# Other durations, latencies and keys for the planner of a fused attention and mixture-of-experts kernel, and one conversion step on another engine

## The chip, the cores and the metric

The kernel runs on one core of one Trainium2 chip. The metric is the time of one execution on the device, in microseconds: the median of 3 runs before the change is 2100.59 us (2096.8 to 2104.3).

The core has a matrix engine (TensorE, PE in the profile), which writes to PSUM only, a vector engine (VectorE, DVE), a scalar engine (ScalarE, ACT), GpSimd (POOL), and SyncE (SP), whose queue issues all DMAs here. Each engine takes its instructions strictly in the order in which the program lists them, and waits on semaphores for the others.

## The reference

Three layers follow one another, all in float32:

```
scores = scale * q k^T;  bias = -(cum[:, None] - cum[None, :]), cum = cumsum(max(s, 0))
attn   = softmax(causal(scores + min(bias, 0)));   x = attn v         # 4 x 8 heads, 576 x 64
P      = exp(x w_gate - max);  8 times: rows, then columns normalised # 2304 tokens, 8 experts
out    = sum over e of P[:, e] * (max(x w1[e], 0) w2[e])              # 512 -> 1024 -> 512
y      = leaky(out w_in) w_out,  leaky(h) = max(0.01 h, h)            # 512 -> 2048 -> 512
```

`w_in` and `w_out` come as float64 and are turned into float32 on the chip.

## The kernel before

**Exact products.** A float32 operand is split into a high part, rounded to the matrix engine's own format by a copy on ScalarE, and a low part, the difference, which VectorE or GpSimd subtracts. Each product then takes three matmuls: high by high, high by low, low by high (lines 294 to 296 for the first layer of an expert, 1054 to 1056 and 1269 to 1271 for the second).

**Seven products for eight.** The first layer of a block (a quarter of an expert's hidden width, 256 columns, on 2 x 384 tokens) is a 2 x 2 block product in the form with seven multiplications P1 to P7. Sums of blocks of the weights and of the inputs go in; additions on VectorE between PSUM banks (line 976, tiles `Uu`, `sc`, `FB`) combine the products afterwards. TensorE starts on a PSUM bank's next product only when these additions have been done.

**Stages.** Attention comes first. Then tokens are taken in three passes (j = 0, 1, 2). A pass runs through 32 units, a unit being a quarter of one of 8 experts. After the three passes, three FF passes of 8 units each compute the last layer. Units are numbered through: 0 to 31 for the first pass, 32 to 63 and 64 to 95 for the second and third, 96 to 119 for the FF passes.

- In the first pass each unit's weights are loaded and split (`weights1`, `weights2`, lines 225 to 277), used, and also stored to DRAM: the seven first-layer operands to `w1c`, the split second-layer blocks to `w2d`, and the unsplit sums of second-layer blocks (`sums`, line 272) to `w2s`. Gating (lines 864 to 935) runs beside units 0 to 3: TensorE computes logits, ScalarE copies them (line 913), TensorE transposes them (line 868), and VectorE normalises.
- From unit 32 on the second layer uses seven products as well. Its operands come from DRAM: `fetch1` (line 1206) brings first-layer operands, `fetch2` (lines 1248 and 1250) second-layer ones. The four that are sums arrive unsplit and `round2` splits them: a cast on ScalarE (line 1255), a subtraction on VectorE (line 1256). There are five buffers, so a fetch waits for the use of the buffer five places earlier. `comb` (line 1230) combines the results of the first layer and `split` (1235 and 1236) splits them, the low parts on GpSimd. `tile2` multiplies and adds to accumulators in `X` (line 1277); `merge` (line 1285) joins these at the end of a pass.
- `conversion` (lines 949 to 956) turns one 128 x 512 piece of `w_in` or `w_out` from float64 bits into float32 by eight VectorE operations. 32 pieces are spread over units: 19 over the first pass from unit 4 on, 13 over the second pass.
- `prepare(u)`, eight times during the third pass, loads a block of the converted `w_in`, forms and splits the first-layer operands, stores them to `w1c`, then does the same with `w_out` for `w2d` and `w2s`. Its VectorE operations stand at line 1355 (a helper) and 272, its casts at 1363, 1367, 1368 and 1378.

**The order of the work.** All that follows attention goes through one planner, `Flow`. `do(engine, key, dur, emit, reads, writes, lat)` adds a task; a task depends on the last writers of what it reads, and on readers and writers of what it writes, by names such as `("w1c", n)`. These names serve the planner; the program's semaphores come from the memory that is touched. `order()` simulates the engines: whenever an engine is free, it takes the ready task with the smallest key. A task is ready when its dependencies have ended and their latency has passed (a table by pair of engines, or `lat` in ns). `dur` is an estimate in ns; `pd`, `pq`, `pa`, `pgg` and `kb` give it from the number of elements (VectorE on SBUF, VectorE reading PSUM, ScalarE, GpSimd, DMA in KB). TensorE's durations are doubled while the plan's clock is under `KEYS["cold"]` = 28 us. A key is in units of the numbering above: 34.5 is the middle of unit 34. The list that results is the order of each engine's queue.

```
now, eng = best
k = min((j for j, (a, _) in enumerate(ready[eng]) if a <= now), key=lambda j: ready[eng][j][1][1])
...
pd = lambda n: 103.0 + n * 1.042
pq = lambda n: 130.0 + n * 1.12
pa = lambda n: 160.0 + n / 1.2
pgg = lambda n: 92.0 + n * 2.3
```

Of the kernel before, what the change touches and what calls it, by code (L numbers as in the profile page):

```python
# [8 lines left out]
F32 = mybir.dt.float32  # L9
# [14 lines left out]
class Plan:  # L24
# [7 lines left out]
    def __init__(self, free=()):  # L32
        self.tasks, self.free = [], dict(free)
# [80 lines left out]
def fused_kernel(ctx: ExitStack, tc: tile.TileContext, q, k, v, s, w_gate, w1, w2, w_in, w_out, out):  # L114
    nc = tc.nc
# [132 lines left out]
    def weights2(n, key):  # L248
# [657 lines left out]
    def gating():  # L906
# [32 lines left out]
    def convert(bits):  # L939
# [9 lines left out]
            lambda: v_.tensor_scalar(out=cva, in0=hi, scalar1=0x7FFFFFFF, scalar2=None, op0=AND),  # L949
# [9 lines left out]
    def conversion(n, key, unit):  # L959
# [6 lines left out]
        for k, f in enumerate(convert(bits)):  # L966
            do("dve", key + 0.11 * k, (370, 370, 370, 370, 640, 370, 640, 640)[k] + 500, f, [br, ("begun", unit)], ["cv"] if k < 7 else ["cv", br])
# [19 lines left out]
    def first(n):  # L987
# [11 lines left out]
        def out(block, bank, key):  # L999
# [37 lines left out]
    def second(n):  # L1037
# [4 lines left out]
        for ch in range(6):  # L1042
# [22 lines left out]
            elif e == 0:  # L1065
                do("dve", k2, pd(512), lambda a=a, y=y: nc.vector.tensor_tensor(out=a, in0=y, in1=a, op=ALU.add), [yr], [ar])
            else:
# [3 lines left out]
                do("dve", k2, pd(512), lambda a=a, y=y, p=p: nc.vector.scalar_tensor_tensor(out=a, in0=y, scalar=p, in1=a, op0=ALU.mult, op1=ALU.add),  # L1071
# [20 lines left out]
    CONVS = {4 + n: 1 for n in range(25) if n % 4 != 3}  # L1092
# [109 lines left out]
    def fetch1(n, o, t):  # L1202
# [3 lines left out]
        do("sp", t, kb(820 if o < NG else 256), lambda: nc.sync.dma_start(out=to.bitcast(F32), in_=src), [("w1c", ci)], [name], 2000)  # L1206
# [36 lines left out]
    def fetch2(q, n, name, t):  # L1243
# [5 lines left out]
        else:  # L1249
            do("sp", t, kb(512), lambda: nc.sync.dma_start(out=to, in_=w2d[ci // 2][:, part - 4]), [("w2d", ci), ("w2d", ci + 1)], names, 2000)  # L1250
# [96 lines left out]
    def prepare(u, t):  # L1347
# [11 lines left out]
        wr = [("w1c", NU1 + u)]  # L1359
        do("sp", t - 0.5, kb(512), lambda: nc.sync.dma_start(out=rawc, in_=win32[:, 256 * u:256 * u + 256].rearrange("(c p) f -> p c f", p=128)), [("in", 4 * c + u // 2) for c in range(4)], [R], 2000)  # L1360
# [4 lines left out]
        do("sp", t + 0.5, kb(512), lambda: nc.sync.dma_start(out=dst[:, 1:5, 0], in_=hf.rearrange("p o k f -> p o (k f)")), [H], wr, 2000)  # L1365
        do("sp", t + 0.5, kb(512), lambda: nc.sync.dma_start(out=dst[:, 1:5, 1], in_=sw.rearrange("p (o f) -> p o f", o=4)), [S_], wr, 2000)
# [4 lines left out]
        do("sp", t + 0.9, kb(256), lambda: nc.sync.dma_start(out=dst[:, 0:6:5, 0], in_=hf[:, 0:2].rearrange("p o k f -> p o (k f)")), [H], wr, 2000)  # L1371
        do("sp", t + 0.9, kb(128), lambda: nc.sync.dma_start(out=dst[:, 6, 0], in_=hf[:, 2].rearrange("p k f -> p (k f)")), [H], wr, 2000)
        for o, src in ((0, A(0, 0)), (5, A(0, 1)), (6, A(1, 1))):
            do("sp", t + 0.9, kb(128), lambda o=o, src=src: nc.sync.dma_start(out=dst[:, o, 1].rearrange("p (k f) -> p k f", k=2), in_=src), [R], wr, 2000)
        raw2 = raw.rearrange("p (c f) -> p c f", c=2)
        do("sp", t + 1.2, kb(512), lambda: nc.sync.dma_start(out=raw2, in_=wout32[256 * u:256 * u + 256, :].rearrange("(c p) f -> p c f", p=128)), [("out", 2 * u + x) for x in range(2)], [R], 2000)
# [9 lines left out]
    for n in range(N0, N1):  # L1386
# [102 lines left out]
```

## Time and profile before

| | before |
|---|---|
| median of 3 runs | 2100.59 us (2096.8 to 2104.3) |
| the profiled execution | 2099.05 us, span 2097.3 us |
| TensorE busy | 2020.6 us, 96% |
| VectorE busy | 1706.9 us, 81% |
| GpSimd busy | 1689.2 us, 81% |
| ScalarE busy | 906.4 us, 43% |
| mean granted TensorE clock | 0.990 |

The span runs from the first to the last instruction of one profiled execution; the execution's own time is a little longer. Busy time of TensorE counts overlapping matmuls once, and a matmul that waits in the pipe counts as busy. How fast TensorE really goes is therefore read from the number of matmuls that pass in a stretch. The granted clock is a share of 2.4 GHz; 0.5 is 1.2 GHz. In the rows, "DVE X L1 <- ACT Y L2" means that VectorE's instruction of line 1, which writes X, waited for ScalarE's of line 2.

### The profile page before, as it was taken

How to read it: one execution, taken by the hardware profiler on the slowest of the kernel's cores; microseconds unless marked ns; L12 is line 12 of the kernel's file. 1: busy time of each engine (PE TensorE's matmuls, PEld its weight loads, DVE VectorE, ACT ScalarE, POOL GpSimd, SP SyncE). 2: the span in 40 equal slices, each digit the busy share in tenths (PEclk: the TensorE clock that was granted, in tenths of full speed). 3: DMA queues.
4: the chain of work that ended last, by engine and by line, in shares of the span. 5: the costliest groups of instructions: out<-in, count | busy, mean ns of one | idle time of the engine just before them, and what ended most of it. 6: DMA issues, size and time to landing. Idle time of an engine off the chain costs nothing. (4 is left out here: it accounts for less than half of the span.)

```text
span 2097.3 us, 34707 instructions
## 1 busy us (share of the span) xinstructions
PE 2020.6 (96%) x11473; PEld 1904.9 (91%) x11473; DVE 1706.9 (81%) x2987; ACT 906.4 (43%) x1896; POOL 1689.2 (81%) x1607
## 2 busy tenths in 40 slices
PE   7999899999999999999999999999999999999998
PEld 5776688888888899999999989989999999999997
DVE  5877489899888879989998988888888885857746
ACT  5888333333332343333333444333333345555553
POOL 7789877888888668888888978777778797978874
PEclk9999999999999999999999999999999999999999
DMA  6664878888889677778776778888888877776663
GB/s 149 139 143 103 307 251 286 290 318 291 298 293 321 231 254 247 250 245 268 247 249 225 245 268 288 285 281 263 294 280 293 277 242 237 234 241 210 221 213 106
DMA packets 303424, 518.17 MB, mean 247 GB/s; under 512 B 81868, under 2 KB 189550, under 8 KB 287886
## 3 DMA queue, kind: packets, MB, share of 16 engines
q1 hardware_dynamic: 303246, 515.96, 74.7%
q8 instruction: 92, 1.51, 0.3%
q14 instruction: 86, 0.70, 0.1%
HBM read 362.11 MB, written 144.05 MB: 241 GB/s over the span
## 5 line engine op out<-in xcount | busy, mean ns | idle before, releaser
L294 PE MATMUL sc<-XO,WQ 128*128 128x384 f32 x960 | 328.3, 342 | 29.7 <-DVE Uu L976 21.6
L295 PE MATMUL sc<-XO,WQ 128*128 128x384 f32 x960 | 323.8, 337 | 0.0
L296 PE MATMUL sc<-XO,WQ 128*128 128x384 f32 x960 | 323.0, 337 | 0.0
L1256 DVE TENSOR_TENSOR WQ<-WQ 128x512 fp32r<-128x512 f32 x176 | 190.7, 1083 | 71.5 <-ACT WQ L1255 71.1
L294 PEld LDWEIGHTS sc<-XO,WQ 128*128 128x128 f32 x960 | 181.6, 189 | 46.7 <-DVE Uu L976 27.6
L295 PEld LDWEIGHTS sc<-XO,WQ 128*128 128x128 f32 x960 | 182.0, 190 | 4.6
L296 PEld LDWEIGHTS sc<-XO,WQ 128*128 128x128 f32 x960 | 182.0, 190 | 0.0
L1255 ACT CAST WQ<-WQ 128x512 fp32r<-128x512 f32 x176 | 109.2, 621 | 162.4 <-DMA WQ<-w2s 143.2
L1277 DVE TENSOR_TENSOR X<-tr,X 128x384 f32<-128x384 f32 x275 | 149.6, 547 | 33.4 <-PE tr L1271 33.1
L294 PE MATMUL FA<-XO,WQ 128*128 128x384 f32 x480 | 161.7, 337 | 0.5 <-DVE GG L1221 0.5
L296 PE MATMUL FA<-XO,WQ 128*128 128x384 f32 x480 | 160.9, 335 | 0.7 <-POOL WQ L225 0.7
L295 PE MATMUL FA<-XO,WQ 128*128 128x384 f32 x480 | 161.1, 336 | 0.0
L976 DVE TENSOR_TENSOR sc<-sc,Uu 128x384 f32<-128x384 f32 x240 | 133.7, 557 | 32.4 <-PE sc L296 31.2
L225 POOL TENSOR_TENSOR WQ<-RB,WQ 128x512 fp32r<-128x512 f32 (+1 forms) x64 | 113.8, 1786 | 28.4 <-ACT WQ L243 17.8
L1236 POOL TENSOR_TENSOR HB<-GG,HB 128x384 fp32r<-128x384 f32 x96 | 108.0, 1128 | 33.9 <-ACT HB L1235 31.0
L1270 PE MATMUL tr<-HB,WQ 128*128 128x384 f32 x307 | 103.1, 336 | 1.2 <-POOL HB L1236 1.2
L1269 PE MATMUL tr<-HB,WQ 128*128 128x384 f32 x307 | 103.1, 336 | 0.1
L1271 PE MATMUL tr<-HB,WQ 128*128 128x384 f32 x307 | 103.0, 335 | 0.0
L1003 ACT ACTIVATE HB<-FB 128x384 fp32r<-128x384 f32 x32 | 15.8, 493 | 201.2 <-DVE FB L976 201.2
L1056 PE MATMUL tr<-WQ,HB 128*128 128x512 f32 x256 | 101.8, 398 | 0.0
L1055 PE MATMUL tr<-WQ,HB 128*128 128x512 f32 x256 | 101.5, 397 | 0.0
L1054 PE MATMUL tr<-WQ,HB 128*128 128x512 f32 x256 | 100.2, 391 | 0.0
(349 smaller groups left out, 6912.8 us busy)
## 6 DMA issues: line engine op xcount, KB each, us to landing
WQ<-w1c SPq DMA_DIRECT2D x88, 1024.0 KB
WQ<-w2d SPq DMA_DIRECT2D x132, 512.0 KB
WQ<-w1c SPq DMA_DIRECT2D x264, 256.0 KB
w1c<-WQ SPq DMA_DIRECT2D x32, 1792.0 KB
WQ<-w2s SPq DMA_DIRECT2D x176, 256.0 KB
w2d<-WQ SPq DMA_DIRECT2D x64, 256.0 KB
w2s<-SS SPq DMA_DIRECT2D x32, 512.0 KB
RB<-in_moe_w_dram SPq DMA_DIRECT2D x16, 512.0 KB
```

Source lines behind the costliest of these rows:

```text
L225: return lambda: nc.gpsimd.tensor_tensor(out=out, in0=x, in1=y, op=op)
L294: nc.tensor.matmul(t, lhsT=hi, rhs=xh, start=new, stop=False, skip_group_check=on)
L295: nc.tensor.matmul(t, lhsT=hi, rhs=xl, start=False, stop=False, skip_group_check=on)
L296: nc.tensor.matmul(t, lhsT=lo, rhs=xh, start=False, stop=(k == 1), skip_group_check=on)
L976: TT = lambda out, x, y: (lambda: v.tensor_tensor(out=out, in0=x, in1=y, op=ALU.add))
L1236: do(eng, t + 0.02, pgg(W) if eng == "pool" else pq(W), lambda: (nc.gpsimd if eng == "pool" else nc.vector).tensor_tensor(out=OP[k][:, 1], ...
L1255: do("act", t, pa(512), lambda: nc.scalar.copy(hi, lo.bitcast(F32)), [("w2l", k)], [("w2h", k)])
L1256: do(eng, t + 0.05, pgg(512) if eng == "pool" else pd(512), lambda: (nc.gpsimd if eng == "pool" else nc.vector).tensor_tensor(out=lo, in0= ...
L1269: nc.tensor.matmul(y[:, 0:W], lhsT=hi, rhs=oh, start=(x == 0), stop=False)
L1270: nc.tensor.matmul(y[:, 0:W], lhsT=hi, rhs=ol, start=False, stop=False)
L1271: nc.tensor.matmul(y[:, 0:W], lhsT=lo, rhs=oh, start=False, stop=(x == 1))
L1277: do("dve", t + 0.08, pq(W), lambda: nc.vector.tensor_tensor(out=a, in0=y[:, 0:W], in1=a, op=ALU.add), [yr], [("A", name, s_)])
```

## The change

It replaces durations, latencies and keys in the planner's input for everything after attention, and takes one operation from VectorE to ScalarE:

- TensorE's durations are no longer doubled at the plan's start. `pd`, `pa`, `pgg` and `kb` get new values; VectorE operations that read PSUM use `pq`; a conversion's operations have new durations.
- The copy of logits has a latency of 4000 ns in the plan instead of 900.
- The first operation of a conversion, the absolute value of the high word, becomes an ACTIVATE with Abs on ScalarE.
- Sums of w2 on GpSimd in the first pass get a key 0.5 units later, `round2` one 0.2 units later. Conversions begin at unit 6 instead of 4, and the later 13 are spread over 28 units instead of 25. `prepare` begins at unit 65.5 instead of 66.5, at 3.4 units' distance instead of 3.2; its first load has a key 0.5 units earlier, and both of its loads a latency of 6000 ns instead of 2000.
- Each store into a `w1c` block, and each into a `w2d` block, gets a name of its own; the fetches read all of them.
- In the last unit the five `comb` subtractions run on VectorE instead of GpSimd.

```diff
-            free[eng] = t[6] = now + t[2] * (2 if eng == "pe" and now < 1000.0 * KEYS["cold"] else 1)
+            free[eng] = t[6] = now + t[2] * (2 if eng == "pe" and now < 1000.0 * self.cold else 1)
...
-        sums(do, n, key + 0.6, raw, r2, SS, "ss", "pool")
+        sums(do, n, key + 1.1, raw, r2, SS, "ss", "pool")
...
     flow = Flow({"pe": 5000.0, "dve": 6000.0})
+    flow.cold = 0.0
-    pd = lambda n: 103.0 + n * 1.042
+    pd = lambda n: 300.0 + n * 1.3
-    pa = lambda n: 160.0 + n / 1.2
+    pa = lambda n: 165.0 + n * 0.87
+    pgg = lambda n: 250.0 + n * 2.1
+    kb = lambda n: n * 3.3
...
-            do("act", k - 1, pa(W), lambda q=q: nc.scalar.copy(G[q % 4], Z[:, 0:W]), ["Z"], [("g", q % 4)], far)
+            do("act", k - 1, pa(W), lambda q=q: nc.scalar.copy(G[q % 4], Z[:, 0:W]), ["Z"], [("g", q % 4)], 4000)
...
-            lambda: v_.tensor_scalar(out=cva, in0=hi, scalar1=0x7FFFFFFF, scalar2=None, op0=AND),
+            lambda: nc.scalar.activation(out=cva.bitcast(F32), in_=hi.bitcast(F32), func=ACTF.Abs),
...
-            do("dve", key + 0.11 * k, (370, 370, 370, 370, 640, 370, 640, 640)[k] + 500, f, [br, ("begun", unit)], ["cv"] if k < 7 else ["cv", br])
+            do("dve" if k else "act", key + 0.11 * k, (620, 870, 940, 1010, 1220, 870, 1060, 1020)[k], f, [br, ("begun", unit)], ["cv"] if k < 7 else ["cv", br])
...
-    CONVS = {4 + n: 1 for n in range(25) if n % 4 != 3}
+    CONVS = {6 + n: 1 for n in range(25) if n % 4 != 3}
...
-        wr = [("w1c", NU1 + u)]
-        do("sp", t - 0.5, kb(512), lambda: nc.sync.dma_start(out=rawc, ...), [("in", 4 * c + u // 2) for c in range(4)], [R], 2000)
+        wr = [[("w1c", NU1 + u, i)] for i in range(7)]
+        do("sp", t - 1.0, kb(512), lambda: nc.sync.dma_start(out=rawc, ...), [("in", 4 * c + u // 2) for c in range(4)], [R], 6000)
...
+        last = "dve" if n == N1 - 1 else "pool"
-        C(1.04, "pool", "T1", 1, 0)
+        C(1.04, last, "T1", 1, 0)
...
-                ev(tq - 0.75, lambda q=q2, t=tq: round2(q, t - 0.75, "dve"))
+                ev(tq - 0.55, lambda q=q2, t=tq: round2(q, t - 0.55, "dve"))
...
-        n = N0 + 2.5 + i * 25.0 / left
+        n = N0 + 2.5 + i * 28.0 / left
-        t = 2 * NU1 + 2.5 + 3.2 * u
+        t = 2 * NU1 + 1.5 + 3.4 * u
```

## Rows read from the trace of the kernel before

**Rows 1.** The page's first part: busy us, share of the span, instructions.
```profile
PE 2020.6 (96%) x11473; PEld 1904.9 (91%) x11473; DVE 1706.9 (81%) x2987; ACT 906.4 (43%) x1896; POOL 1689.2 (81%) x1607
```
**Rows 2.** Busy time by stretch: length, each engine's busy us (instructions), clock, DMA.
```profile
215.00:250.00 35.00, 28.56 (x164) 20.60 (x163) 11.34 (x28) 13.74 (x27) 31.14 (x34) 0.95 0.82 292
310.00:360.00 50.00, 45.82 (x216) 39.43 (x215) 45.99 (x65) 15.00 (x25) 39.63 (x35) 0.97 0.85 292
360.00:735.00 375.00, 371.14 (x1845) 331.97 (x1844) 336.72 (x492) 124.32 (x215) 304.90 (x266) 1.00 0.83 290
735.00:1195.00 460.00, 459.52 (x2643) 456.62 (x2642) 413.13 (x656) 170.02 (x337) 385.46 (x342) 1.00 0.74 247
1195.00:1260.00 65.00, 59.83 (x332) 58.87 (x332) 57.09 (x86) 28.17 (x56) 53.37 (x45) 0.97 0.83 273
1195.00:1760.00 565.00, 538.40 (x3024) 530.93 (x3024) 468.60 (x746) 225.44 (x439) 447.73 (x400) 0.98 0.83 276
1760.00:2000.00 240.00, 235.55 (x1370) 233.62 (x1369) 166.56 (x240) 131.20 (x271) 195.97 (x176) 1.00 0.69 227
2000.00:2097.30 97.30, 87.69 (x493) 85.62 (x491) 55.41 (x92) 41.57 (x86) 63.18 (x62) 0.96 0.47 152
1000.00:1050.00 50.00, 50.00 (x291) 50.00 (x290) 47.84 (x78) 17.07 (x34) 42.53 (x39) 1.00 0.78 262
```
**Rows 3.** TensorE's waits, 1195 to 1760: us in total, times, longest.
```profile
PE sc L294 <- DVE Uu L976: 18.6, 12, 2.8
```
**Rows 4.** VectorE's waits, 1195 to 1760.
```profile
DVE WQ L1256 <- ACT WQ L1255: 19.2, 20, 2.8
...
DVE CV L272 <- DMA CV<-wout: 8.2, 6, 3.6
...
DVE CV L1355 <- DMA CV<-win: 4.3, 3, 1.7
```
**Rows 5.** ScalarE's waits, 1195 to 1760.
```profile
ACT WQ L1255 <- DMA WQ<-w2s: 58.6, 39, 5.9
```
**Rows 6.** In order of time from 1377: start, us, engine, operation [idle before].
```profile
1377.77 4.12 DVE L272 TENSOR_TENSOR CV<-CV 128x256 f32<-128x256 f32 x4 [0.73 <-DMA CV<-wout]
...
1384.19 0.44 PE L294 MATMUL sc<-XO,WQ 128*128 128x384 f32 x1 [1.51 <-DVE Uu L976]
```
**Rows 7.** Groups by line and shape: busy us, mean ns | idle before.
```profile
L1256 DVE TENSOR_TENSOR WQ<-WQ 128x512 fp32r<-128x512 f32 x176 | 190.7, 1083 | 71.5 <-ACT WQ L1255 71.1
...
L1255 ACT CAST WQ<-WQ 128x512 fp32r<-128x512 f32 x176 | 109.2, 621 | 162.4 <-DMA WQ<-w2s 143.2 <-PE FA L296 10.5 <-PE Y L1270 2.3
...
L949 DVE TENSOR_SCALAR CV<-CV 128x512 uint32<-128x512 uint32 x32 | 40.8, 1275 | 0.0
L1355 DVE TENSOR_TENSOR CV<-CV 128x256 f32<-128x256 f32 x40 | 34.6, 891 | 4.6 <-DMA CV<-win 4.3
...
L1355 DVE TENSOR_TENSOR CV<-CV 128x1024 f32<-128x1024 f32 x16 | 23.6, 1473 | 0.8 <-ACT CV L1363 0.2
```
**Rows 8.** In order of time, gating, from 233.
```profile
233.26 1.04 ACT L243 CAST WQ<-RB 128x1024 fp32r<-128x1024 f32 x1 [6.00 <-POOL RB L225]
...
234.74 0.55 PE L868 MATMUL tr<-ident,GG 128*128 128x128 f32 x3 [4.08 <-ACT GG L913]
```
**Rows 9.** VectorE in order of time, from 322.
```profile
322.34 1.00 DVE L956 TENSOR_TENSOR CV<-CV 128x512 f32<-128x512 f32 x1
...
323.74 2.16 DVE L1070 TENSOR_SCALAR acc<-acc,P 128x512 f32<-128x512 f32 x1
```
**Rows 10.** Line 949 (ns min/median/max), and ScalarE's only table load.
```profile
L949 DVE TENSOR_SCALAR CV<-CV x32: 419/1199/2429, 286.2 to 1098.3; 128x512 uint32<-128x512 uint32 x32
...
L422 ACT ACT_TABLE_LOAD x1 | 1.3, 1283 | 0.7 <-PEq L1473 0.7
```
**Rows 11.** The tail in order of time, from 2079.
```profile
2079.46 3.27 DVE L1285 TENSOR_TENSOR X<-X 128x384 f32<-128x384 f32 x6
...
2083.25 0.44 PE L1269 MATMUL Y<-RB,WQ 128*128 128x384 f32 x1 [3.38 <-DVE X L1277]
```

More of the change, by code (lines that the diff above doesn't have):

```diff
@@ L32, in __init__ @@
     def __init__(self, free=()):
-        self.tasks, self.free = [], dict(free)
+        self.tasks, self.free, self.cold = [], dict(free), KEYS["cold"]
     def add(self, eng, key, dur, emit, deps=(), lat=None):
@@ L256, in weights2 @@
         do("pool", key + 0.5, pgg(1024), sub(wb[1], raw, wb[0].bitcast(F32), ALU.subtract), [r2, ("vh", s)], [("vl", s)])
-        do("sp", key + 0.9, kb(1430), lambda: nc.sync.dma_start(out=w1c[n], in_=WQ.bitcast(F32)[:, s, 0:2 * NA]), [(x, s) for x in ("wh0", "wl0", "wh4", "wl4", "wh6", "wl6")], [("w1c", n)], 2000)
+        do("sp", key + 0.9, kb(1430), lambda: nc.sync.dma_start(out=w1c[n], in_=WQ.bitcast(F32)[:, s, 0:2 * NA]), [(x, s) for x in ("wh0", "wl0", "wh4", "wl4", "wh6", "wl6")], [("w1c", n, 0)], 2000)
         for a in range(2):
             direct(do, n, key + 0.8, a, wb[a].bitcast(F32), ("v" + "hl"[a], s))
-        sums(do, n, key + 0.6, raw, r2, SS, "ss", "pool")
+        sums(do, n, key + 1.1, raw, r2, SS, "ss", "pool")
     def direct(do, n, key, a, half, name):
         to = w2d[n // 2][:, :, a, n % 2, :]
-        do("sp", key, kb(256), lambda: nc.sync.dma_start(out=to[:, 0:2], in_=half[:, 0:2, 0:256]), [name], [("w2d", n)], 2000)
-        do("sp", key, kb(128), lambda: nc.sync.dma_start(out=to[:, 2], in_=half[:, 1, 256:512]), [name], [("w2d", n)], 2000)
+        do("sp", key, kb(256), lambda: nc.sync.dma_start(out=to[:, 0:2], in_=half[:, 0:2, 0:256]), [name], [("w2d", n, a, 0)], 2000)
+        do("sp", key, kb(128), lambda: nc.sync.dma_start(out=to[:, 2], in_=half[:, 1, 256:512]), [name], [("w2d", n, a, 1)], 2000)
     def sums(do, n, key, raw, rr, to, name, eng):
@@ L1065, in second @@
             elif e == 0:
-                do("dve", k2, pd(512), lambda a=a, y=y: nc.vector.tensor_tensor(out=a, in0=y, in1=a, op=ALU.add), [yr], [ar])
+                do("dve", k2, pq(512), lambda a=a, y=y: nc.vector.tensor_tensor(out=a, in0=y, in1=a, op=ALU.add), [yr], [ar])
             else:
@@ L1070, in second @@
                     do("dve", k2 - 0.02, pdd(512), lambda a=a, p0=p0: nc.vector.tensor_scalar(out=a, in0=a, scalar1=p0, scalar2=None, op0=ALU.mult), ["P"], [ar])
-                do("dve", k2, pd(512), lambda a=a, y=y, p=p: nc.vector.scalar_tensor_tensor(out=a, in0=y, scalar=p, in1=a, op0=ALU.mult, op1=ALU.add),
+                do("dve", k2, pq(512) + 40, lambda a=a, y=y, p=p: nc.vector.scalar_tensor_tensor(out=a, in0=y, scalar=p, in1=a, op0=ALU.mult, op1=ALU.add),
                    [yr, "P"], [ar])
@@ L1205, in fetch1 @@
         src = w1c[ci][:, 0:512 * NG] if o < NG else w1c[ci][:, 512 * o:512 * o + 512]
-        do("sp", t, kb(820 if o < NG else 256), lambda: nc.sync.dma_start(out=to.bitcast(F32), in_=src), [("w1c", ci)], [name], 2000)
+        do("sp", t, kb(820 if o < NG else 256), lambda: nc.sync.dma_start(out=to.bitcast(F32), in_=src), [("w1c", ci, i) for i in range(7)], [name], 2000)
     def prod(n, name, t):
@@ L1249, in fetch2 @@
         else:
-            do("sp", t, kb(512), lambda: nc.sync.dma_start(out=to, in_=w2d[ci // 2][:, part - 4]), [("w2d", ci), ("w2d", ci + 1)], names, 2000)
+            do("sp", t, kb(512), lambda: nc.sync.dma_start(out=to, in_=w2d[ci // 2][:, part - 4]), [("w2d", ci + x, a, i) for x in range(2) for a in range(2) for i in range(2)], names, 2000)
     def round2(q, t, eng):
@@ L1358, in prepare @@
         R, S_, H = ("f", 0), ("f", 1), ("f", 2)
[L1359 to L1360 removed]
+        wr = [[("w1c", NU1 + u, i)] for i in range(7)]
+        do("sp", t - 1.0, kb(512), lambda: nc.sync.dma_start(out=rawc, in_=win32[:, 256 * u:256 * u + 256].rearrange("(c p) f -> p c f", p=128)), [("in", 4 * c + u // 2) for c in range(4)], [R], 6000)
         for i, (o, x, y, op) in enumerate(((S[:, 0], A(1, 0), A(1, 1), ALU.add), (S[:, 1], S[:, 0], A(0, 0), ALU.subtract), (S[:, 2], A(0, 0), A(1, 0), ALU.subtract), (S[:, 3], A(0, 1), S[:, 1], ALU.subtract))):
@@ L1370, in prepare @@
         do("dve", t + 0.8, pd(256), TT(A(1, 1), A(1, 1), hf[:, 2], ALU.subtract), [H], [R])
[L1371 to L1374, printed above, removed]
+        do("sp", t + 0.9, kb(256), lambda: nc.sync.dma_start(out=dst[:, 0:6:5, 0], in_=hf[:, 0:2].rearrange("p o k f -> p o (k f)")), [H], wr[2], 2000)
+        do("sp", t + 0.9, kb(128), lambda: nc.sync.dma_start(out=dst[:, 6, 0], in_=hf[:, 2].rearrange("p k f -> p (k f)")), [H], wr[3], 2000)
+        for w_, (o, src) in zip(wr[4:], ((0, A(0, 0)), (5, A(0, 1)), (6, A(1, 1)))):
+            do("sp", t + 0.9, kb(128), lambda o=o, src=src: nc.sync.dma_start(out=dst[:, o, 1].rearrange("p (k f) -> p k f", k=2), in_=src), [R], w_, 2000)
         raw2 = raw.rearrange("p (c f) -> p c f", c=2)
-        do("sp", t + 1.2, kb(512), lambda: nc.sync.dma_start(out=raw2, in_=wout32[256 * u:256 * u + 256, :].rearrange("(c p) f -> p c f", p=128)), [("out", 2 * u + x) for x in range(2)], [R], 2000)
+        do("sp", t + 1.2, kb(512), lambda: nc.sync.dma_start(out=raw2, in_=wout32[256 * u:256 * u + 256, :].rearrange("(c p) f -> p c f", p=128)), [("out", 2 * u + x) for x in range(2)], [R], 6000)
         sums(do, NU1 + u, t + 1.6, raw2, R, sw.rearrange("p (k f) -> p k f", k=4), S_, "dve")
@@ L1417, in fused_kernel @@
         S(0.90, "pool", "P2", 2)
-        C(1.04, "pool", "T1", 1, 0)
-        C(1.06, "pool", 1, 3, 1)
+        C(1.04, last, "T1", 1, 0)
+        C(1.06, last, 1, 3, 1)
         S(1.08, "pool", "P5", "T1")
-        C(1.10, "pool", "T2", 3, "T1")
+        C(1.10, last, "T2", 3, "T1")
         S(1.14, "pool", "P7", 1)
         S(1.18, "pool", "P6", "T2")
-        C(1.22, "pool", 2, 2, "T2")
+        C(1.22, last, 2, 2, "T2")
         S(1.26, "pool", "P4", 2)
```

6 lines of the change are left out of this document (3 added, 3 removed).

## The prediction

> **What bounds the kernel now.** I read the page's busy times first, then busy time by stretch, then who waited for whom in the stretches that lose most, then single rows in order of time. TensorE is busy 96% of the span [rows 1], so at most some 77 us of idle can be won, plus what it loses at half clock. At full pace 291 matmuls of 384 columns pass in the 50 us from 1000: 0.172 us each [rows 2]. Held against this, the stretches say where the time goes:
> - 735 to 1195 (second pass): 0.5 us of 460 idle. Nothing to win.
> - 1195 to 1760 (third pass, in which the FF weights are prepared): 3024 matmuls x 0.172 = 520 us, in 565: 45 us lost. Of these 565 - 538.4 = 27 us are idle; at a mean clock of 0.98 about 0.02 x 565 = 11 us go at 1.2 instead of 2.4 GHz; the rest is slow first matmuls.
> - 215 to 250 (gating): 6.4 us idle + 0.05 x 35 = 1.8 us of clock, 8.2 lost. 310 to 360 (units 5 to 8): 4.2 + 0.03 x 50 = 5.7 lost. The rest of the first pass: 3.9 idle.
> - 1760 to 2000: 240 - 1370 x 0.172 = 4.4 lost. The tail after 2000: 9.6 idle + 0.04 x 97 = 13.5, much of it the last merges, which nothing can cover.
>
> In the worst stretch TensorE waits for VectorE's additions at line 976, 12 times, 18.6 us [rows 3]; VectorE itself has work for only 83% of it (468.6 of 565). So it isn't short of capacity there: it stands in its own queue. Its waits: 19.2 us for the rounding of w2 sums on ScalarE (line 1255), 8.2 and 4.3 us for the two loads of a preparation step [rows 4]. ScalarE stands in the same way, 58.6 us, 39 times, for the sums to land [rows 5]. One case in order of time: the queue waits 0.73 us for a load, runs four 256-element operations in 4.12 us, and the addition that TensorE needs comes behind them; TensorE idles 1.51 us [rows 6].
>
> **The change part by part.** The whole second half is put in order by a list planner, so new durations and new keys move everything after 215 us; attention keeps its own plan and durations, and I leave its 215 us alone.
>
> *Rounding moved from 0.75 to 0.55 units before use.* The fetch stays at 1.2 units. A unit takes 84 matmuls x 0.172 = 14.5 us, so a sum gets 0.2 x 14.5 = 2.9 us more to land. ScalarE's mean wait is 58.6 / 39 = 1.5 us [rows 5], so most go; longer ones (to 5.9) are only cut. I take two thirds of VectorE's 19.2 us: 13 us. What is left before use is (0.55 + 0.07) x 14.5 = 9 us, less 0.62 on ScalarE and 1.08 on VectorE [rows 7]: 7.3 us of slack for queueing.
>
> *Preparation.* Loads get half a unit (7.3 us) more lead and the planner allows 6 us instead of 2 for them; the waits on them, at longest 3.6 and 1.7 us [rows 4], go: 12.5 us. The seven stores into one w1c block lose a chain that exists only in the planner; their issues on SP come closer together and the next load is no longer held behind them in the plan. The planner's duration for a VectorE operation on SBUF goes from 103 + 1.042n to 300 + 1.3n ns: 370 to 633 for 256 elements (trace 891), 636 to 966 for 512 (trace 1083) [rows 7]. So it no longer believes that VectorE is free for such blocks when it isn't, and an addition that is ready sooner gets its place ahead of them. It can't cut a 4 us block that has begun, and the operations stay as long as they are.
>
> Together 13 + 12.5 = 25.5 of 31.7 us of those VectorE waits vanish. Not each is a TensorE stall, and blocks like that of [rows 6] remain in part: I value the stretch's gain at 0.7 x 25.5 = 18 us of its 45. Bounds: a loss of 10 (a different order makes as many new stalls as half of those that it removes) and a gain of 38 (it becomes as clean as the second pass).
>
> *Gating.* TensorE waits 4.08 us for a ScalarE copy which stands behind a weight conversion, itself 6.00 us behind GpSimd [rows 8]. The planner is now told 4 us for this copy instead of 0.9, so TensorE gets other work ahead of the transposes. Against it, TensorE's time is no longer doubled in the plan's first 28 us, which until now kept it from running ahead of its suppliers. I take 5 of 8.2; bounds 0 and 8.
>
> *Conversions begin at unit 6 instead of 4.* At the turn of units 4 and 5 six multiplications of line 1070 run between the pieces of a conversion; one takes 2.16 us, behind a 1.00 us piece [rows 9], and TensorE stalls there. Two conversions less there take some 2 x 8.2 us off VectorE (8 pieces; the first alone has a mean of 1.275 [rows 7]). I take 3.5 of 5.7; bounds 0 and 5.7.
>
> *Absolute value on ScalarE.* VectorE loses 32 x 1.275 = 40.8 us; ScalarE gains 32 x about 0.62 = 20 us (a 512-element cast of line 1255, the nearest row [rows 7]) where it is busy 124 of 375 us [rows 2]. The 13 later conversions lie where TensorE is full already: nothing. The 19 of the first pass ease an engine that is busy 337 of 375 us; with the w2 sums on GpSimd half a unit later (no TensorE wait hangs on them) I take 1 of the 3.9 us; bounds -4 and 3.9. If the function needed a table of its own, each conversion would add up to two loads of 1.28 us [rows 10] on ScalarE, 82 us in all, 2.6 in a unit of some 15 us that leaves it two thirds idle: inside the lower bound.
> The Trainium skill ("ScalarE: Activation LUTs", Rules for kernel authors) speaks against this move: cheap functions belong on VectorE, which it has as the faster engine for them. The shortest of these operations, 419 ns [rows 10], agrees with the rule, their mean does not; by the rule the move would gain nothing and the 1 us would go. The same page (Table sets) puts abs in every set, by which no load is added; no run so far shows it.
>
> *Last unit's combinations on VectorE.* Five operations leave GpSimd; but TensorE's wait in the tail, 3.38 us, is for an addition behind six merges on VectorE [rows 11], and VectorE gets more work. I take 0.5; bounds -3 and 3.
>
> *1760 to 2000*: a truer plan, 1 of 4.4. *Second pass*: 0, bounds -6 and 0.5, as its cover is a VectorE that is 90% busy.
>
> Sum: 18 + 5 + 3.5 + 1 + 0.5 + 1 = 29 us. The profiled execution took 2099.05 (span 2097.3); the median, 2100.59, is 1.5 above it. 2099.05 - 29 + 1.5 = 2071.6, so 2072.
>
> **The rivals.**
> (a) *The waits go and the stalls stay*: VectorE's long blocks, not its waits, decide, and beside gating and units 5 to 8 (5 + 3.5) the stretch gains 2.5 of the 18, 11 in all: 2090. For it: the block of [rows 6] took 4.12 us after a wait of only 0.73. Against it: waits fill 31.7 us of a stretch that loses 45.
> (b) *Nearly all is won*: 38 + 8 + 5.7 with the rest as above (2.5), 54: 2047. Against it: the merges and the next pass's operands at 1195 to 1260 cost 65 - 332 x 0.172 = 7.9 us whatever the order.
> (c) *No change*: gains and new stalls cancel, 2100. For it: the second pass is full only by this very order.
> (d) *Slower: roundings come late.* The slack of 7.3 us is eaten where VectorE runs behind, and TensorE, which never waits for line 1256 now, waits for it. It decides where VectorE's queue lags more than 7.3 us; the first preparation, moved up one unit to the turn of the pass, adds 12 us of work (nine operations of 256 elements at 0.89, one of 512 at 1.1, two of 1024 at 1.47 [rows 7]) where VectorE is busy 57 of 65 us [rows 2]. 44 late roundings, one in four, at 1 us each cost 44 us, against 29 gained: 2116. Against it: the longest load wait of VectorE is 3.6 us, half the slack.
>
> **How the numbers follow.** The forecast (2056 to 2082) 0.47, (b) 0.12, (a) 0.18, (c) 0.09, (d) 0.14. About 0.3% (6.3 us) is what can be told from no change here. Faster: 0.47 + 0.12 + 0.18 = 0.77; same 0.09; slower 0.14. Eight in ten: from 2048 (half of (b) outside) to 2104 (all of (d) outside).
>
> **What would show it.** In the changed profile: ScalarE's wait for the landing sums under a third of its 143 us [rows 7]; VectorE's waits for the preparation's loads near nothing; TensorE's waits for line 976 between 1195 and 1760 down from 18.6 to about 10, clock there back to 0.99; the 4.08 us wait in gating gone; no idle at 310 to 360. Wrong if TensorE waits for line 1256, if the second pass shows idle, or if those VectorE waits go and the stretch still loses 40 us.

## The result and the profile after

The changed kernel takes 2052.68 us (median of 4 runs, 2050.90 to 2056.72), the kernel before 2102.43 beside it (4 runs, 2096.80 to 2104.30): a ratio of 0.977, 95% interval 0.9745 to 0.9795. The profiled execution took 2050.9 us, span 2049.1, against 2099.05 and 2097.3. Lines 816 to 1414 of the old kernel stand three lines lower in the new one (913 is 916, 976 is 979, 1256 is 1259, 1355 is 1358).

The page's busy times, which answer to [rows 1]:

```profile
PE 2005.9 (98%) x11473; PEld 1899.5 (93%) x11473; DVE 1644.7 (80%) x2959; ACT 923.9 (45%) x1928; POOL 1686.6 (82%) x1603
```

TensorE has the same 11473 matmuls in 14.7 us less busy time; VectorE has 28 instructions and 62 us less (the 32 absolute values went to ScalarE, and four subtractions of the last unit came from GpSimd: four by the count and by the edit, where the text on the change and the prediction say five). Busy time by stretch, columns as in [rows 2]:

```profile
215.00:250.00 35.00, 31.96 (x190) 24.50 (x190) 12.70 (x28) 14.59 (x28) 32.29 (x32) 1.00 0.90 331
310.00:360.00 50.00, 50.00 (x252) 44.96 (x251) 45.19 (x69) 18.90 (x32) 42.37 (x39) 1.00 0.83 290
360.00:735.00 375.00, 375.00 (x1875) 336.85 (x1874) 318.51 (x483) 136.22 (x234) 302.91 (x267) 1.00 0.86 299
735.00:1195.00 460.00, 460.00 (x2658) 459.66 (x2656) 395.05 (x651) 176.89 (x352) 396.79 (x350) 1.00 0.77 250
1195.00:1260.00 65.00, 61.22 (x347) 59.62 (x346) 57.35 (x89) 31.59 (x63) 55.03 (x49) 1.00 0.88 295
1195.00:1760.00 565.00, 557.32 (x3199) 553.85 (x3198) 481.07 (x771) 244.27 (x479) 478.66 (x425) 1.00 0.85 285
1760.00:2000.00 240.00, 236.99 (x1381) 235.55 (x1380) 156.21 (x236) 133.71 (x276) 198.45 (x179) 1.00 0.69 225
```

Matmuls in the same 565 us rise from 3024 to 3199, the granted clock there from 0.98 to 1.00: the part at 1.2 GHz is gone. But the work slides through these fixed windows. So the account below goes by units instead: a unit starts with the first of its four matmuls of line 294 into the bank `FA`, of which there are 480. Us between starts, from the one profiled execution of each kernel (the lower lines are the experiments of the next section):

```
                    start   units                                            last
                    of 0    0-3   4-7   8-31   32-63  64-103 104-118 unit  span
before              200.1   84.0  70.2  380.7  463.9  623.5  229.7   45.3  2097.3
after               201.4   78.8  63.7  376.2  462.4  593.2  227.8   45.5  2049.1
a_round75           204.2   78.7  63.7  376.2  462.4  595.2  227.0   45.2  2052.7
b_olddur            200.9   78.4  64.3  381.7  463.0  609.4  229.8   45.5  2073.0
c_duronly           203.3   79.9  69.3  378.5  466.3  602.2  227.0   45.1  2071.5
d_noabs             201.2   78.3  63.7  381.3  465.3  594.9  227.3   45.3  2057.4
e_prepback          201.7   78.4  63.7  376.2  462.4  599.4  227.5   45.6  2055.0
f_gateback          203.1   81.1  62.9  376.2  462.5  594.2  227.4   45.6  2052.9
g_convback          200.6   78.4  68.9  376.0  464.7  595.4  227.7   45.7  2057.5
i_oldpd             199.8   78.5  63.7  376.2  462.4  607.6  230.0   46.0  2064.2
h_lastpool          199.7   78.3  63.7  376.2  462.4  593.8  227.9   44.9  2046.9
j_preptime          200.4   78.4  63.7  376.2  462.6  599.5  227.4   44.9  2053.0
k_pdonly            200.6   84.0  68.1  376.4  467.9  603.7  229.1   44.5  2074.2
m_pdhigh            199.8   78.4  63.7  376.1  467.6  617.3  227.9   45.2  2076.0
```

Of 48.2 us of span, 30.3 come in units 64 to 103 (third pass and first FF pass, with the preparation), 5.2 in units 0 to 3 (gating), 6.5 in units 4 to 7, 4.5 in 8 to 31, 1.5 in the second pass, 1.9 in 104 to 118; the last unit gives nothing. The stretch of units 64 to 103 by itself, before and then after:

```profile
1198.80:1822.30 623.50, 596.90 (x3362) 589.43 (x3361) 510.16 (x805) 258.49 (x506) 497.71 (x445) 0.99 0.81 271
...
1182.60:1775.80 593.20, 585.52 (x3361) 582.05 (x3361) 505.97 (x805) 258.98 (x506) 506.10 (x446) 1.00 0.85 285
```

With the same matmuls, TensorE's idle time falls from 26.6 to 7.7 us, which is 18.9 of the 30.3. Before the change TensorE also ran at 1.2 GHz for five short pieces of this stretch, 17 us together, which cost some 8.5 us; after it for none.

How far one execution can be trusted shows in two of the experiments, f_gateback and h_lastpool. There every engine's order in these units is that of the changed kernel, but for one or two instructions of VectorE, and they take 594.2 and 593.8 us against 593.2. The first holds one piece at 1.2 GHz, which costs 1.7 us; g_convback, d_noabs and j_preptime hold one each as well. So differences under 2 us in this stretch are not read as effects. One such piece, of the kernel before, right behind TensorE's stall of 2.8 us that ended at 1401.83, and one of f_gateback (the clock is the third number from the end):

```profile
1402.50:1405.90 3.40, 3.40 (x12) 3.40 (x11) 3.40 (x6) 1.02 (x2) 1.55 (x2) 0.50 0.99 388
...
1223.00:1226.00 3.00, 3.00 (x9) 3.00 (x10) 2.96 (x6) 1.71 (x4) 1.86 (x2) 0.50 0.98 365
```

Who waits in units 64 to 103 of the new kernel (us, times, longest; 1182 to 1776):

```profile
DVE WQ L1259 <- ACT WQ L1258: 14.3, 11, 2.3
...
PE sc L294 <- DVE RAW L1224: 2.1, 1, 2.1
...
PE tr L1274 <- DVE WQ L1259: 0.7, 1, 0.7
...
PE sc L294 <- DVE Uu L979: 0.4, 1, 0.4
```

TensorE's 12 stalls for the additions [rows 3] are down to one of 0.4 us. VectorE's waits for a preparation's loads [rows 4] are gone; its wait for the rounding is 14.3 us. The same units of the kernel before (1198 to 1822) had:

```profile
DVE WQ L1256 <- ACT WQ L1255: 28.5, 26, 2.8
...
PE sc L294 <- DVE Uu L976: 18.6, 12, 2.8
```

Groups by line and shape of the new kernel, as in [rows 7]: busy us, mean ns, idle before.

```profile
L1259 DVE TENSOR_TENSOR WQ<-WQ 128x512 fp32r<-128x512 f32 x176 | 175.0, 996 | 49.6 <-ACT WQ L1258 49.1
L1258 ACT CAST WQ<-WQ 128x512 fp32r<-128x512 f32 x176 | 109.4, 622 | 222.8 <-DMA WQ<-w2s 190.5 <-PE FA L296 13.8 <-PE tr L1274 6.6
...
L1358 DVE TENSOR_TENSOR CV<-CV 128x256 f32<-128x256 f32 x40 | 36.8, 927 | 0.1
...
L952 ACT ACTIVATE CV<-CV 128x512 f32<-128x512 f32 x32 | 21.7, 677 | 0.0
```

ScalarE's wait for the landing sums did not fall: it rose from 143.2 to 190.5 us. The absolute value takes 677 ns on ScalarE, where it took 1275 on VectorE.

The preparation in order of time. First a block of the same line as the 4.12 us of [rows 6], then one of the first half of a preparation step:

```profile
1387.99 3.85 DVE L272 TENSOR_TENSOR CV<-CV 128x256 f32<-128x256 f32 x4
...
1358.41 0.87 DVE L1358 TENSOR_TENSOR CV<-CV 128x256 f32<-128x256 f32 x1
...
1360.14 1.57 DVE L1358 TENSOR_TENSOR CV<-CV 128x256 f32<-128x256 f32 x2
```

The four operations of line 272 still run as one, in all eight steps (seven before the change). Those of line 1358 ran as one in six steps before the change and do so in none now: in the example an operation each of lines 1224 and 1280, which work on products, lie between the first and the next two.

Gating, for [rows 8]: the ScalarE copy at 234.06 is used by the transposes only 4 us after its end, and nobody waits for it.

```profile
234.06 0.47 ACT L916 COPY GG<-Z 128x384 f32<-128x384 f32 x1
...
238.55 0.49 PE L871 MATMUL Y<-ident,GG 128*128 128x128 f32 x3
```

The tail, for [rows 11]: the stall of 3.38 us is still there, to the hundredth.

```profile
2034.95 0.51 PE L1272 MATMUL Y<-RB,WQ 128*128 128x384 f32 x1 [3.38 <-DVE X L1280]
```

### The profile page after: what moved, and what is told of

Same layout as the page of the kernel before. It is cut to its first block, busy times and chain, and to the rows that moved or that the text cites. A ratio compares the mean times of both kernels' runs of the same rounds, so it can differ in the third digit from the quotient of the medians.

```text
span 2049.1 us, 34649 instructions
## 1 busy us (share of the span) xinstructions
PE 2005.9 (98%) x11473; PEld 1899.5 (93%) x11473; DVE 1644.7 (80%) x2959; ACT 923.9 (45%) x1928; POOL 1686.6 (82%) x1603
## 5 line engine op out<-in xcount | busy, mean ns | idle before, releaser
L294 PE MATMUL sc<-XO,WQ 128*128 128x384 f32 x960 | 322.4, 336 | 3.2 <-DVE RAW L1224 2.1
L295 PE MATMUL sc<-XO,WQ 128*128 128x384 f32 x960 | 321.4, 335 | 0.0
L296 PE MATMUL sc<-XO,WQ 128*128 128x384 f32 x960 | 321.3, 335 | 0.0
L1259 DVE TENSOR_TENSOR WQ<-WQ 128x512 fp32r<-128x512 f32 x176 | 175.0, 996 | 49.6 <-ACT WQ L1258 49.1
L1258 ACT CAST WQ<-WQ 128x512 fp32r<-128x512 f32 x176 | 109.4, 622 | 222.8 <-DMA WQ<-w2s 190.5
L1280 DVE TENSOR_TENSOR X<-tr,X 128x384 f32<-128x384 f32 x275 | 150.5, 550 | 46.4 <-PE tr L1274 44.9
L979 DVE TENSOR_TENSOR Uu<-sc,Uu 128x384 f32<-128x384 f32 x120 | 66.1, 551 | 49.4 <-PE sc L296 48.7
```

The source lines that it names most:

```text
L294: nc.tensor.matmul(t, lhsT=hi, rhs=xh, start=new, stop=False, skip_group_check=on)
L295: nc.tensor.matmul(t, lhsT=hi, rhs=xl, start=False, stop=False, skip_group_check=on)
L296: nc.tensor.matmul(t, lhsT=lo, rhs=xh, start=False, stop=(k == 1), skip_group_check=on)
L979: TT = lambda out, x, y: (lambda: v.tensor_tensor(out=out, in0=x, in1=y, op=ALU.add))
L1258: do("act", t, pa(512), lambda: nc.scalar.copy(hi, lo.bitcast(F32)), [("w2l", k)], [("w2h", k)])
L1259: do(eng, t + 0.05, pgg(512) if eng == "pool" else pd(512), lambda: (nc.gpsimd if eng == "pool" else nc.vector).tensor_tensor(out=lo, in0= ...
```

## The experiments

Three groups of four kernels; the kernel before beside them took 2100.16, 2101.03 and 2100.11 us. Each ratio is to that. "After" stands for the changed kernel, 2052.68.

After the result two theories stood. K is the prediction's own step: the keys do it, that is the later rounding and the preparation's loads, whose waits on VectorE go. D: the planner's truer durations do it, which the prediction named but gave no price of its own. The first group sets them against each other.

**a_round75**: the changed kernel with the rounding back at 0.75 units before use.

```diff
-ev(tq - 0.55, lambda q=q2, t=tq: round2(q, t - 0.55, "dve"))
+ev(tq - 0.75, lambda q=q2, t=tq: round2(q, t - 0.75, "dve"))
```

> The changed kernel with the w2 sums rounded 0.75 units before use again, nothing else undone. Theory K (the keys carry the gain: sums and loads get time to land): some 9 us of the 30 won in units 64 to 103 go back, total near 2062, and ScalarE's wait for the landing sums rises well above the changed kernel's 190 us. Theory D (the planner's truer durations carry it, because ready additions are no longer listed behind blocks that the plan takes for short): within 3 us of the changed kernel, 2050 to 2056.

2053.97 (2051.96 to 2056.35), ratio 0.9783, 0.9761 to 0.9806. Units 64 to 103 lose 2.0 us. The waits in them, and behind them ScalarE's wait for the sums over the whole run, here and in f_gateback, which has the new key:

```profile
DVE WQ L1259 <- ACT WQ L1258: 16.4, 14, 2.8
...
PE sc L294 <- DVE Uu L979: 0.4, 1, 0.4
```

```profile
ACT WQ L1258 <- DMA WQ<-w2s: 201.2, 119, 5.3
...
ACT WQ L1257 <- DMA WQ<-w2s: 204.5, 119, 4.8
```

ScalarE's wait, 201.2 us with the old key and 190.5 in the changed kernel, shows no clear effect of the later key: f_gateback has 204.5 with the new one. VectorE's wait for the rounding rises from 14.3 to 16.4 us only. In the changed kernel the key is worth 2 us at most, not 13: K falls for the rounding there. What it is worth under the old durations no run tells.

**b_olddur**: the changed kernel with all old durations of the second half.

```diff
-    pd = lambda n: 300.0 + n * 1.3
+    pd = lambda n: 103.0 + n * 1.042
-    pa = lambda n: 165.0 + n * 0.87
-    pgg = lambda n: 250.0 + n * 2.1
-    kb = lambda n: n * 3.3
+    pa = lambda n: 160.0 + n / 1.2
...
```

> The changed kernel with the old duration formulas for VectorE, ScalarE, GpSimd and DMA and the old durations of a conversion's operations; all keys, names, latencies and the operation on ScalarE stay changed. Theory D: units 64 to 103 lose 20 us or more again and TensorE waits for line 979 come back there, the first pass loses some 4, total 2075 to 2085. Theory K: within 6 us of the changed kernel, 2050 to 2059.

**c_duronly**: the kernel before with the new durations alone.

```diff
-    pd = lambda n: 103.0 + n * 1.042
+    pd = lambda n: 300.0 + n * 1.3
-    pa = lambda n: 160.0 + n / 1.2
+    pa = lambda n: 165.0 + n * 0.87
+    pgg = lambda n: 250.0 + n * 2.1
+    kb = lambda n: n * 3.3
...
```

> The kernel before with the new durations alone. Theory D: units 64 to 103 win 20 us or more, total 2072 to 2082, with gating and the turn of units 4 and 5 as slow as before. Theory K: less than 8 us are won, total 2094 or more. If both are needed together, neither this kernel nor the one with the old durations comes near the changed one.

b: 2075.24 (2072.34 to 2079.67), ratio 0.9886, 0.9861 to 0.9911. c: 2073.86 (2072.34 to 2075.08), ratio 0.9878, 0.9852 to 0.9904. Durations alone gain 26 us, everything else alone 25, both together 48 to 50: over the whole run they nearly add up. In units 64 to 103 they overlap: 21.3 us for the durations alone and 14.1 for the rest alone, against 30.3. Waits in units 64 to 103, b first, then c:

```profile
DVE WQ L1257 <- ACT WQ L1256: 35.7, 23, 4.0
...
PE sc L294 <- DVE Uu L977: 11.7, 10, 2.8
```

```profile
DVE WQ L1258 <- ACT WQ L1257: 15.3, 17, 2.3
...
DVE CV L1357 <- DMA CV<-win: 9.7, 6, 4.0
...
PE sc L294 <- DVE Uu L978: 6.1, 9, 0.9
...
DVE CV L272 <- DMA CV<-wout: 5.6, 6, 1.7
```

This pair is crossed. In b VectorE no longer waits for loads, yet TensorE still stalls for 11.7 us, up to 2.8 at a time. In c it waits 15.3 us for loads, more than the 12.5 of [rows 4], and TensorE stalls 6.1 us, never over 0.9. So TensorE's stalls do not follow VectorE's waits for loads. Nor does the later key, with the old durations of b, shorten VectorE's waits for the rounding: they are 35.7 us, 28.5 before the change.

**d_noabs**: the changed kernel with the absolute value on VectorE again.

```diff
-            lambda: nc.scalar.activation(out=cva.bitcast(F32), in_=hi.bitcast(F32), func=ACTF.Abs),
+            lambda: v_.tensor_scalar(out=cva, in0=hi, scalar1=0x7FFFFFFF, scalar2=None, op0=AND),
```

> The changed kernel with a conversion's first operation back on VectorE. If the 24 us that this puts back on VectorE in the first pass matter (19 operations of 1.275 us, where VectorE is busy 85%): units 5 to 31 lose 3 to 6 us, total 2056 to 2059. If the operation is hidden anyway: within 1.5 us, 2051 to 2054, and the first pass still runs without an idle TensorE.

2058.93 (2057.08 to 2062.73), ratio 0.9809, 0.9786 to 0.9832: 6.2 us more than after. Units 8 to 31 lose 5.1 us, the second pass 2.9, units 64 to 103 1.7, no more than the one piece at 1.2 GHz that d has there. Busy time from 360 to 735, against the third line of the table by stretch; first d, then b_olddur and k_pdonly:

```profile
360.00:735.00 375.00, 372.32 (x1847) 331.36 (x1847) 347.36 (x495) 124.53 (x215) 303.04 (x264) 1.00 0.84 297
...
360.00:735.00 375.00, 371.79 (x1846) 330.64 (x1845) 338.09 (x480) 130.70 (x231) 302.95 (x262) 1.00 0.83 295
...
360.00:735.00 375.00, 374.90 (x1866) 336.03 (x1866) 334.51 (x494) 126.73 (x217) 303.12 (x265) 1.00 0.84 294
```

With VectorE at 347 of 375 us instead of 319, TensorE gets through 1847 matmuls instead of 1875. But the operation's engine is not all that counts here: b has it on ScalarE and the old durations, and takes 381.7 us for units 8 to 31; k below has it on VectorE and the new `pd`, and takes 376.4, as good as after. The 5.1 us are what the move is worth within the changed plan; a truer plan without it wins nearly as much.

The second and third groups take the change apart further. **i_oldpd** and **k_pdonly** single out one formula, the duration of a VectorE operation on SBUF (`pd`): i is the changed kernel with the old formula, k the kernel before with the new one (and the three operations that read PSUM priced by `pq`, as after has them: 703 instead of 636 ns for 512 elements).

```diff
-    pd = lambda n: 300.0 + n * 1.3      # i; in k the other way round
+    pd = lambda n: 103.0 + n * 1.042
```

> The changed kernel with the old formula for VectorE operations on SBUF alone (103 + 1.042n instead of 300 + 1.3n ns); all other durations, keys and latencies stay changed. Theory P (it is this formula, which had the blocks of the preparation and the rounding's subtraction at some 60% of their traced length): the loss is that of the kernel with all old durations, units 64 to 103 lose some 16 us, total 2068 to 2076. Theory Q (the other durations, GpSimd's above all, carry a good part): units 64 to 103 lose less than 8, total under 2064.

> The kernel before with only that formula new, and with the additions that read PSUM planned by their own formula. Theory P: nearly what all the new durations give, units 64 to 103 win 18 to 21 us, total 2074 to 2082. Theory Q: under half of it, total 2088 or more.

i: 2065.11 (2063.70 to 2065.99), ratio 0.9833, 0.9807 to 0.9859. k: 2076.18 (2075.28 to 2078.06), ratio 0.9889, 0.9867 to 0.9911. In units 64 to 103, i loses 14.4 of the 30.3 us and k wins 19.8. TensorE's stalls for the additions in these units in i, and then the waits in k:

```profile
PE sc L294 <- DVE Uu L979: 8.6, 6, 2.4
```

```profile
DVE WQ L1256 <- ACT WQ L1255: 22.4, 22, 2.2
...
DVE CV L272 <- DMA CV<-wout: 6.3, 5, 2.7
...
DVE CV L1355 <- DMA CV<-win: 4.8, 4, 1.7
...
PE sc L294 <- DVE Uu L976: 4.3, 4, 1.4
```

In k one formula, with the three operations priced by `pq`, takes TensorE's stalls from 18.6 to 4.3 us, while VectorE keeps most of its waits (22.4 of 28.5 us for rounding, 11.1 of 12.5 for loads).

**m_pdhigh**: is it truth that helps, or merely caution? The changed kernel with durations well above the trace (1319 ns for 512 elements, trace 996).

```diff
-    pd = lambda n: 300.0 + n * 1.3
+    pd = lambda n: 500.0 + n * 1.6
```

> The changed kernel with 500 + 1.6n ns for VectorE operations on SBUF: 910 ns for 256 elements (traced mean 927), 1319 for 512 (traced 996), 2138 for 1024 (traced 1464). Theory truth (the gain comes from durations near the mean that is traced): the longer shapes are now 30 to 45% too long in the plan, some of the 14 to 20 us goes, total 2057 to 2065. Theory caution (any plan that leaves a margin around these operations does): no loss or a further gain, 2047 to 2055.

2081.99 (2077.74 to 2087.45), ratio 0.9908, 0.9878 to 0.9938. Units 64 to 103 lose 24.1 us, the second pass 5.2: it is not caution that helps. The stalls are of another kind, on several chains at once, while VectorE waits less for the rounding than in any other kernel here:

```profile
DVE WQ L1259 <- ACT WQ L1258: 4.9, 5, 1.8
...
PE tr L1272 <- ACT SS L1238: 4.8, 1, 4.8
PE Y L1272 <- DVE X L1280: 4.5, 1, 4.5
PE sc L294 <- ACT RAW L1226: 3.2, 1, 3.2
PE sc L294 <- DVE Uu L979: 2.0, 1, 2.0
```

"Truth" holds for the longer shapes only. The changed kernel's formula gives 633 ns for 256 elements (trace 927), 966 for 512 (996), 1631 for 1024 (1464); that of m gives 910, 1319 and 2138. So m has the 256-element operations right, which the changed kernel still has a third too short, and loses all the same. The 176 roundings have 512 elements; no run changes the price of one shape alone.

**e_prepback** and **j_preptime**: e is the changed kernel with all of the preparation's edits undone (start and distance, lead and latency of the loads, the chain of the stores); j undoes start and distance alone.

```diff
-        t = 2 * NU1 + 1.5 + 3.4 * u          # e and j
+        t = 2 * NU1 + 2.5 + 3.2 * u
-        do("sp", t - 1.0, kb(512), ... [R], 6000)      # e only, and so for the second load
+        do("sp", t - 0.5, kb(512), ... [R], 2000)
-        wr = [[("w1c", NU1 + u, i)] for i in range(7)] # e only, and its reader
+        wr = [[("w1c", NU1 + u, 0)]] * 7
```

> The changed kernel with the preparation's start and distance (66.5, 3.2), its loads' keys and latencies (2 us) and the chain of its w1c stores as before; durations stay new. If these carry the rest of the gain in units 64 to 103 (9 us, the difference between all durations alone and the whole change): 9 us lost there, VectorE waits some 15 us for the preparation's loads again, total 2060 to 2064. If VectorE's waits for loads don't reach TensorE once the durations are right: within 3 us, 2051 to 2056.

> The changed kernel with the preparation's start and distance alone as before (66.5, 3.2); its loads keep their lead and latency, its stores their own names. If the first preparation, moved up to the turn of the pass, costs there (units 64 to 67 take 63.4 us where others take 58.2): some 2 to 4 us faster in units 64 to 103, total 2049 to 2052. If the greater distance is what helps: 2 to 4 us slower, 2055 to 2058.

e: 2054.46 (2054.35 to 2056.76), ratio 0.9787, 0.9766 to 0.9809. j: 2053.43 (2051.78 to 2058.34), ratio 0.9774, 0.9741 to 0.9807. The medians put e 1.8 and j 0.8 us behind after, less than they can tell. In the account units 64 to 103 lose 6.2 us in e and 6.3 in j: by that start and distance carry it, the load edits and the unchained stores nothing that can be told. The 6.2 may be high: the profiled execution is the slowest of e's four and the fastest of after's. The waits of e in these units:

```profile
DVE CV L1358 <- DMA CV<-win: 12.9, 7, 2.8
DVE WQ L1259 <- ACT WQ L1258: 12.5, 11, 3.5
...
DVE CV L272 <- DMA CV<-wout: 5.6, 6, 1.6
...
PE sc L294 <- DVE Uu L979: 2.4, 4, 1.0
```

VectorE's 18.5 us of waits for loads are back, more than before the change; j has none, and takes as long.

**f_gateback**: the 900 ns for the gating copies and the doubled matmuls of the plan's first 28 us are back.

```diff
-    flow.cold = 0.0
...
-[("g", q % 4)], 4000)
+[("g", q % 4)], far)
```

> The changed kernel with TensorE's planned durations doubled up to 28 us again and 0.9 us instead of 4 as the latency of the logits' copy. If these two carry the 5.2 us won in units 0 to 3: they go, TensorE waits for line 916's copy up to some 4 us, total 2056 to 2060. If the new durations of GpSimd and ScalarE are what moved the copy: less than 2 us are lost, 2051 to 2055.

2054.85 (2052.00 to 2055.76), ratio 0.9784, 0.9762 to 0.9806. Units 0 to 3 lose 2.3 us; TensorE waits for the copies again (200 to 290):

```profile
PE tr L870 <- ACT GG L915: 3.4, 2, 2.3
```

The other half of gating's 5.2 us stays, since durations other than `pd` win there too: c, with all of them and without these two edits, brings these units to 79.9 us; k, with `pd` alone, leaves them at 84.0. And b, with the old durations and everything else changed, has 78.4. Either gives nearly all of it; the two overlap.

**g_convback**: conversions from unit 4 again, and the later 13 over 25 units instead of 28.

```diff
-    CONVS = {6 + n: 1 for n in range(25) if n % 4 != 3}
+    CONVS = {4 + n: 1 for n in range(25) if n % 4 != 3}
...
-        n = N0 + 2.5 + i * 28.0 / left
+        n = N0 + 2.5 + i * 25.0 / left
```

> The changed kernel with conversions from unit 4 on again and the later 13 over 25 units. If these two conversions less at the turn of units 4 and 5 carry the 6.5 us won in units 4 to 7: 4 to 6.5 of it go back, total 2056 to 2060. If VectorE's new order and its lighter conversions are enough there: under 2 us, 2051 to 2055.

2056.57 (2056.24 to 2059.30), ratio 0.9789, 0.9763 to 0.9814. Units 4 to 7 lose 5.2 us of their 6.5, the second pass 2.3. TensorE's longest wait from 278 to 355 is back on VectorE:

```profile
PE sc L294 <- DVE HB L1007: 2.0, 1, 2.0
```

**h_lastpool**: the last unit's combinations on GpSimd again.

```diff
-        last = "dve" if n == N1 - 1 else "pool"
+        last = "pool"
```

> The changed kernel with the last unit's five combinations on GpSimd again. The forecast's 0.5 us: within 1 us, 2051.5 to 2055, the time after the start of unit 119 at 45 to 46 us as in both kernels. If GpSimd's chain did bound the tail, 3 to 5 us later, the start of unit 119 unchanged.

2049.04 (2047.69 to 2053.09), ratio 0.9753, 0.9727 to 0.9779. The last unit takes 44.9 us against 45.5, its stall of 3.4 us for an addition stays: no effect. The lower median is not shown to be a gain of this edit: the interval overlaps that of after, and in the profiled execution 1.7 us of the 2.2 lie ahead of unit 0, where the two kernels have the same instructions.

## Why the prediction was right, and where it was not

Faster, as forecast; at 2052.7 it is 19 us below the predicted 2072, inside the range, below the forecast's own 2056 and 6 above rival (b). Of the signs that it named, TensorE's waits, the clock, gating and the loads came out; ScalarE's wait did not. By stages:

- *Gating*, 5 foreseen, 5.2 measured; the wait of [rows 8] is gone. Right in size and place; but the durations alone, which the prediction had not named for it, give 4.1 of it too (c); the rest of the change without them (b) gives 5.6.
- *Units 4 to 7*, 3.5 foreseen, 6.5 measured; 5.2 of it by the conversions' later start (g). The upper bound was 5.7, taken from one window of 50 us; the stretch that gained is longer.
- *Absolute value*, 1 foreseen, with bounds up to 3.9; 5.1 us in units 8 to 31 when it is undone (d), though k has nearly the whole gain there without it. And nothing for the 13 later conversions was wrong: they bring 2.9 us in the second pass (d). An idle of 0.5 us in 460 was the wrong measure for that: it is the idle of one order, and the order of the changed plan would lose there without them (d 2.9 us against after, k 4.0 against before). No table load was added: 32 operations, 677 ns in the mean.

  The Trainium skill ("ScalarE: Activation LUTs", Rules for kernel authors) has relu, max, min, add and mul on VectorE rather than ScalarE, and gives VectorE's advantage for bf16. The prediction read that more widely: the row names neither the absolute value nor 32-bit words. Here the operation takes 677 ns on ScalarE against 1275 on VectorE in the mean, and undoing the move costs 6.2 us by the medians.
- *Units 104 to 118*, 1 foreseen for 1760 to 2000, 1.9 measured, not taken apart. *Last unit*, 0.5 foreseen, nothing measured (h).
- *Units 64 to 103*, the large term: 18 foreseen for 1195 to 1760, 30.3 measured in these units. **Here the step failed.** It read "13 + 12.5 = 25.5 of 31.7 us of those VectorE waits vanish" and valued the stretch at 0.7 of that. The load waits did go, but by the runs the load edits and stores are worth about nothing (e less j); the later rounding takes VectorE's wait for it from 16.4 to 14.3 us instead of down by two thirds, and is worth 2.0 us at most (a). ScalarE's wait for the sums was to fall below a third of 143 us; it is 190.5. In place of that step: `pd` 14.4 to 19.8 us (i, k), start and distance of the preparation up to 6.2 (e, j), rounding up to 2.0. Together these come to some 23 to 28 of the 30.3 us. Each was found by undoing one part of the changed kernel, or for k by adding it to the old one.

  That the time still fell into the range is partly luck. The prediction named the truer durations and gave them no price; without them the kernel takes 2075 (b), near the forecast of 2072, and with them the 18 us that had been worked out from vanishing waits came from elsewhere. Why the rest of the change wins 14.1 us in these units under the old durations is not taken apart.

Rival (a) had the better cause: the blocks of VectorE, not its waits, decide. Of the 12 stalls of [rows 3], nine have 1.6 to 4.1 us of the preparation's operations on VectorE in the 5 us before TensorE goes on, the three others, 1.7 us in all, roundings; only four have a wait of VectorE there. But (a) concluded that the stalls would therefore stay. They went when the formula alone was changed (k), and came back with the old one (i), with 8.6 us. The likely reason is that the list planner places the additions by the lengths that it believes: with 370 ns for an operation that takes 891, it believes a block of four to be over in 1.5 us when it takes up to 4. The new 633 ns makes that 2.5, nearer and still short.

How the truer order does it in detail stays open. That other work splits the blocks, as in the example above, is not it: unbroken runs of four 256-element operations number 13 of 16 in before, 15 in c, k and e, 8 in after, and 9 in b and i. c, k and e keep whole blocks and lose most of the stalls; b and i split nearly all of line 1358's and have stalls of 11.7 and 8.6 us. The split comes with what e undoes and j does not, the loads' edits and the stores' names, and is worth nothing that shows. ScalarE's longer wait comes in good part with the durations: 129.2 us with the old ones (b), 156.7 with the old `pd` alone (i), 190.5 after; and 169.2 in k against 143.2 before. How a truer `pd` lengthens it is open.

Rival (d), roundings that come late, did not occur: TensorE waits once for line 1259, for 0.7 us. By the letter that was one of the prediction's signs of being wrong, and it was set too strictly. What is left in the third pass is mostly its turn: units 64 to 67 take 63.4 us, the other fours of the pass 58.2 to 60.3.

## What to carry to other kernels

An engine's waits are not the price of what it delivers: take the instructions that lay ahead of the late one in its queue, and ask what put them there. Where a planner writes the order, compare its durations with the means of the trace before anything else; here a formula that was 41% short at 512 elements cost 14 to 20 us of 2050, and one that was a third too long there cost 24. An account between fixed events of the program (starts of units) places terms of 2 to 6 us that medians with a spread of 5 can't; take more than one execution, or kernels with the same order in a stretch, to learn its noise.

## What the runs showed that was not expected

- Stages repeat far better than whole runs. Units 8 to 31 took 376.0 to 376.2 us in nine kernels of the account, in four of them with another order than after's there: TensorE is busy without a gap in that stretch (375.00 of 375 us after), so its pace is the floor. By contrast the start of unit 0 moves between 199.7 and 204.2 us although attention's instructions are the same in all fourteen. How much of the totals' spread starts there is not measured: each kernel has one trace.
- The same instruction's mean moves with the order: line 1256/1259 went from 1083 to 996 ns, the 256-element operations of line 1355/1358 from 891 to 927. A planner's duration is the mean of one order only.
